# Cosine attention and a gated MLP in one kernel: neighbouring heads as a pair, norms in PSUM, roots by GpSimd's power, a new plan

## The chip, the cores and the metric

The kernel runs on one core of one Trainium2 chip. The core has a matrix engine (TensorE, PE in the profile, with its weight loads as PEld), a vector engine (VectorE, DVE), an engine for functions (ScalarE, ACT), a general one (GpSimd, POOL) and a queue engine that issues transfers (SyncE, SP); 16 DMA engines move data between the main memory, the on-chip memory SBUF and, through no DMA, the accumulation memory PSUM, which has eight banks. The engines run side by side, each through its own list of instructions in order, and wait for each other by semaphores. The metric is the device time of one execution in microseconds.

## The reference

Attention with normalised queries and keys over 8 batches of 12 heads, 448 positions and 64 columns, then a product with a gate over all 3584 tokens:

```python
def _attn_ref(q, k, v, tau):
    q_n = q / (np.linalg.norm(q, axis=-1, keepdims=True) + 1e-06)
    k_n = k / (np.linalg.norm(k, axis=-1, keepdims=True) + 1e-06)
    scores = np.matmul(q_n, k_n.transpose(0, 1, 3, 2)) / tau
    scores = scores - np.max(scores, axis=-1, keepdims=True)
    attn = np.exp(scores)
    attn = attn / (np.sum(attn, axis=-1, keepdims=True) + 1e-09)
    return np.matmul(attn, v)

def _moe_ref(x, w_in, w_out):          # 768 -> 2048 -> 768
    h = x @ w_in
    g = h * (1.0 / (1.0 + np.exp(-1.702 * h)))
    return g @ w_out

# attention out (8, 12, 448, 64) -> x (3584, 768), heads side by side
```

`tau` is 0.1. Everything comes and goes as float32; the kernel multiplies in float16.

## The kernel before, in words

**Tiling.** The unit of attention is a duo y: four heads of one batch, so three duos a batch (`ND = 3`) and 24 in all. A load (L217) puts the four heads' q, or k, into one tile `qk32` of 128 partitions: a head's 448 positions are 64 partitions of 7 positions each, two heads stand one above the other in the partitions, and two such stacks lie side by side (index j). So partitions 0 to 63 hold heads 0 and 2, partitions 64 to 127 heads 1 and 3 of the duo. After the transposes a pair of heads that is worked on together is what stood in one half of the partitions: heads 0 and 2, or 1 and 3. The rows of `w_in` are therefore not in their natural order on chip: `load_w_in` (L594) brings them in eight transfers that put the rows of each pair where the attention's result will be. v has four transfers a duo (L230), of 64 partitions each.

**Steps of a duo.** Squares (L243 on ACT, L242 on POOL for batch 1), sums over the 64 columns (L249, DVE), then the norm. In batch 0 that is a root by logarithm and exponential on ACT (L260, L261), and on DVE an addition of 1e-6 and a reciprocal (L265, L266), for q and k each by itself. From batch 1 it is `norm_a` and `norm_b`: a first guess of the inverse root from the bits of the number (L273), two Newton steps of three instructions (L286 to L290), and the correction for the 1e-6 (L297 to L301), ten DVE instructions; from batch 2 the second and third duo of a batch share one group. `scale` (L316) multiplies q or k by its inverse norm and writes float16: k of batch 0 and everything later on POOL, k in two pieces because its positions are placed in another order, q of batch 0 on DVE. Then q and k are turned: for the first six duos (`TURNED`) by PE (L339), with a DVE copy out of PSUM (L350), and the last 64 keys, which are treated by themselves, copied into the tile `kL` on DVE (L356); later by DMA transposes on SP (L362) with the `kL` copies on POOL (L371). PE makes the scores (L381, and L407 for the last keys), ACT the exponentials (L416), PE multiplies by v (L444, L455; v is cast to float16 into the tiles `vt` on POOL, L327 and L333, and carries a column of ones that yields the sums), DVE divides (L467, L475), and the result is turned to `xT` (L485 and L495, or a DMA transpose L503). Batch 0 is worked in two halves of its queries so that the product can begin early.

**The product.** L513 (L543 for batch 0) multiplies by `w_in`, ACT takes a tanh (L523), DVE the gate (L530, L555), L568 multiplies by `w_out`, ACT halves into `ost` (L579), SP stores (L589). The product of a batch is spread between the attention of the next ones.

**What sets the order.** A planner (`Plan`) simulates the engines when the program is built: every step has an engine, an assumed duration, a due time, steps that must be over before it, and counted buffers that it takes and frees. At each moment a free engine takes the ready step with the earliest due time. The order that results is what each engine's list holds; on the chip an engine waits in place at an instruction whose inputs are late, and everything behind it in its list waits too. `early` is the due time of squares, sums and norms; `hold` keeps the q, k and v loads of later batches until `w_in` or `w_out` have landed. The counted buffer `port` keeps POOL's steps and some of DVE's apart; `mm` counts the four PSUM banks for results, `sp` the two double banks for scores. Loads are issued in the order of their due times (`turn`). Eight semaphores serve the transfers of SP and ACT by turns, so the transfer that is issued eight later waits until the earlier has landed.

**The start.** DVE sets each of the six `vt` tiles to zero and writes its ones (L790 to L793), then clears the ends of the three `exp` tiles and the three `kL` tiles (L795, L796).

Of the kernel before, what the change touches and what calls it, by code (L numbers as in the profile page):

```python
# [10 lines left out]
FP32 = mybir.dt.float32  # L11
FP16 = mybir.dt.float16
I32 = mybir.dt.int32
# [4 lines left out]
RS_MAGIC = float(0x5F1FFFF9)  # L18
RS_A, RS_B = 0.703952253, 0.703952253 * 2.38924456
# [125 lines left out]
def kernel(  # L145
# [50 lines left out]

    ctx.enter_context(tc.manual_schedule())

    ident = const.tile([128, 128], FP16)
    w_in_sb = wpool.tile([128, KT1, DFF], FP16, name="w_in")  # L200
    w_out_sb = wpool.tile([128, KT2, DM], FP16, name="w_out")
    vts = [const.tile([128, 4, 2, D + 1], FP16, name=f"vt{i}") for i in range(NV)]
    exps = [const.tile([128, 2, EW], FP16, name=f"exp{i}") for i in range(NE)]
    kLs = [const.tile([128, 2, 128], FP16, name=f"kL{i}") for i in range(NE)]
# [9 lines left out]
    def load(y, d, src, nm):  # L214
        b, h0 = y // ND, (y % ND) * 4
        d[y] = p_in.tile([128, 2, C, D], FP32, name="qk32")
        return (nc.scalar if d is q32 and y == 0 else nc.sync).dma_start(  # L217
            out=d[y].rearrange("p j c d -> p j (c d)"),
            in_=src[b, h0 : h0 + 4]
            .rearrange("h s d -> (h s d)")  # L220
            .rearrange("(j q f) -> q j f", j=2, f=C * D),
        )

    def load_v(y, j, half):
        b, h0 = y // ND, (y % ND) * 4 + 2 * j
        if j + half == 0:
# [5 lines left out]
            in_=v[b, h0 : h0 + 2].rearrange("g (p c) d -> p g (c d)", c=C)[:, :, D * c0 : D * (c0 + n)],  # L232
        )

    def on_pool(y, ti):
        return y // ND == 1

# [7 lines left out]
    def reduce(y, ti):  # L245
        grp = group_of[y]
        if grp not in n2s:
            n2s[grp] = p_n.tile([128, len(grp), 2, 2, C], FP32, name=f"n2_{len(grp)}")
        nc.vector.tensor_reduce(  # L249
            out=n2s[grp][:, y - grp[0], ti],  # L250
# [5 lines left out]
    def root(y, ti):  # L256
        if y not in rss:
            rss[y] = p_n.tile([128, 2, 2, C], FP32, name="rs", bufs=4)
        n = n2s[group_of[y]][:, 0, ti]
        nc.scalar.activation(out=n, in_=n, func=AF.Ln)  # L260
        return nc.scalar.activation(out=n, in_=n, func=AF.Exp, scale=0.5)  # L261

    def invert(y, ti):
        n = n2s[group_of[y]][:, 0, ti]
        nc.vector.tensor_scalar(out=n, in0=n, scalar1=1e-6, scalar2=None, op0=ALU.add)  # L265
        return nc.vector.reciprocal(out=rss[y][:, ti], in_=n)  # L266

    def norm_a(grp):
        n = len(grp)
        a = n2s.pop(grp).rearrange("p g a b c -> p (g a b c)")  # L270
        y = p_n.tile([128, 4 * C * n], FP32, name=f"y_{n}")
        t = p_n.tile([128, 4 * C * n], FP32, name=f"t_{n}")
        nc.vector.tensor_scalar(  # L273
            out=y.bitcast(I32),
            in0=a.bitcast(I32),
            scalar1=-0.5,
            scalar2=RS_MAGIC,
            op0=ALU.mult,
            op1=ALU.add,
        )  # L280
        nrms[grp] = a, y, t
        return newton(grp, RS_A, RS_B)

    def newton(grp, ca, cb):
        a, y, t = nrms[grp]
        nc.vector.scalar_tensor_tensor(  # L286
            out=t, in0=y, scalar=-ca, in1=y, op0=ALU.mult, op1=ALU.mult
        )
        nc.vector.tensor_tensor(out=t, in0=t, in1=a, op=ALU.mult)
        return nc.vector.scalar_tensor_tensor(  # L290
            out=y, in0=t, scalar=cb, in1=y, op0=ALU.add, op1=ALU.mult
        )

    def norm_b(grp):
        newton(grp, 0.5, 1.5)
        a, y, t = nrms.pop(grp)
# [544 lines left out]
```

## Time and profile before

| | us |
|---|---|
| three runs | 445.81, 447.77, 452.8 (median 447.77) |
| the profiled execution | 453.23 |
| its span on the core | 451.5 |
| PE busy, share of the span | 414.7, 92% |
| ACT busy | 275.0, 61% |
| DVE busy | 233.1, 52% |
| POOL busy | 149.7, 33% |
| first score on PE | at 17.09 |
| first product of batch 0 (L543) | at 40.12 |
| DMA queue of SP and ACT (q1), share of 16 engines | 52.8% |

The span is the time from the first to the last instruction of the profiled execution. A line of the time line gives start and duration in microseconds, engine, source line, operation, output and inputs, and in brackets how long the engine had been idle just before and what released it. In a group of equal instructions the two numbers behind the bar are the busy time in all and the mean of one in nanoseconds; behind the second bar stands the idle time before them. The granted clock of PE was 0.991 in the mean. A matrix product counts as busy until its modelled end.

### The profile page before, as it was taken

The page shows a single profiled execution, that of the slowest core. Times are in us where ns is not written, and L with a number is a line of the kernel's source. Part 1 is how long each engine was busy: PE and PEld are TensorE (multiplying, and loading weights), DVE is VectorE, ACT ScalarE, POOL GpSimd, SP SyncE. Part 2 cuts the span into 40 slices and gives each one's busy share as a digit, 9 for nine tenths or more (in the row PEclk, how much of TensorE's full clock was granted, in tenths as well). Part 3 has the DMA queues.
Part 4 walks back from the last instruction along what each step waited for, and adds up shares of the span by engine and source line. Part 5 has one row for each costly group of instructions (what it writes and reads, how often), then busy time and mean ns, then how long its engine had stood idle before and what let it go on. Part 6 is the DMA issues. An engine that isn't in the chain of part 4 may idle for free.

```text
span 451.5 us, 9300 instructions
## 1 busy us (share of the span) xinstructions
PE 414.7 (92%) x3614; PEld 249.9 (55%) x3614; DVE 233.1 (52%) x605; ACT 275.0 (61%) x417; POOL 149.7 (33%) x271
## 2 busy tenths in 40 slices
PE   0589799999889999889999999799999999999995
PEld 0367677654456555455555555365555655565563
DVE  7835988796755755652664444571353115503400
ACT  5568476858877776764786565775666556324321
POOL 2666665556475174017421624017120000000000
PEclk9999899999999999999999999899999999999999
DMA  8798398999998888728864499337501321021022
GB/s 293 143 219 252 110 191 204 266 203 257 145 195 188 221 230 157 155 92 187 173 157 142 114 197 200 81 103 136 123 13 22 81 55 46 12 70 36 1 71 70
DMA packets 85996, 63.33 MB, mean 140 GB/s; under 512 B 54080, under 2 KB 80960, under 8 KB 85952
## 3 DMA queue, kind: packets, MB, share of 16 engines
q1 hardware_dynamic: 81936, 55.99, 52.8%
q0 software_dynamic: 3744, 6.29, 8.0%
q8 instruction: 28, 0.46, 0.4%
q10 hardware_dynamic: 272, 0.46, 0.3%
q14 instruction: 16, 0.13, 0.1%
HBM read 45.61 MB, written 11.01 MB: 125 GB/s over the span
## 4 chain that ended last, share of the span: by engine, by line
PE 66%; DMA 10%; POOL 6%; SPq 6%; issue 5%; DVE 4%; ACT 3%; POOLq 0%; ACTq 0%; DVEq 0%
PE mm L568 29%; PE mm L513 24%; PE mm L455 5%; PE sp L381 5%; DMA qk<-in_k_dram 4%; SPq L230 4%; DMA v<-in_v_dram 3%; POOL qks L316 3%; PE mm L444 2%; ACT exp L416 2%; PE sp L407 1%; DMA out_dram<-ost 1%; DMA qkT<-qks 1%; POOL sq L242 1%; SPq L217 1%
## 5 line engine op out<-in xcount | busy, mean ns | idle before, releaser
L416 ACT ACTIVATE exp<-sp 128x896 f16<-128x896 f32 (+1 forms) x171 | 148.2, 905 | 38.0 <-PE sp L381 32.8
L568 PE MATMUL mm<-w_out,gT 128*128 128x384 f16 x896 | 155.5, 326 | 1.6 <-DVE gT L530 1.4
L513 PE MATMUL mm<-xT,w_in 128*128 128x448 f16 x672 | 137.3, 354 | 0.9 <-DVE xs L475 0.9
L568 PEld LDWEIGHTS <-gT 128*128 128x128 f16 x896 | 84.3, 98 | 64.1 <-issue 9.5
L530 DVE SCALAR_TENSOR_TENSOR gT<-th,mm 128x448 f16<-128x448 f16 x112 | 68.5, 617 | 62.7 <-ACT th L523 62.6
L523 ACT ACTIVATE th<-mm 128x448 f16<-128x448 f32 x128 | 69.5, 548 | 51.4 <-PE mm L513 41.0
L513 PEld LDWEIGHTS <-w_in 128*128 128x128 f16 x672 | 62.8, 98 | 65.0 <-issue 9.1
L316 POOL TENSOR_TENSOR qks<-qk,y 128x512 f16<-128x512 f32 (+2 forms) x63 | 73.0, 1188 | 11.5 <-issue 5.3
L249 DVE TENSOR_REDUCE n<-sq 128x14 f32<-128x896 f32 x48 | 51.4, 1078 | 36.5 <-ACT sq L243 36.4
L455 PE MATMUL mm<-vt,exp 128*128 128x65 f16 (+1 forms) x1152 | 60.8, 197 | 1.8 <-ACT exp L416 1.8
L455 PEld LDWEIGHTS <-exp 128*128 128x128 f16 (+1 forms) x1152 | 54.1, 101 | 13.0 <-issue 5.4
L327 POOL CAST vt<-v 128x384 f16<-128x384 f32 x48 | 24.3, 506 | 109.2 <-PE mm L455 41.1
L579 ACT ACTIVATE ost<-mm 128x384 f32<-128x384 f32 x56 | 27.2, 492 | 49.9 <-PE mm L568 43.6
L243 ACT ACTIVATE sq<-qk 128x896 f32<-128x896 f32 x42 | 39.6, 950 | 28.3 <-DMA qk<-in_k_dram 21.7
L467 DVE RECIPROCAL rc<-mm 112x4 f32<-112x4 f32 x96 | 17.1, 178 | 68.7 <-PE mm L455 68.6
L444 PE MATMUL mm<-vt,exp 128*128 128x130 f16 x192 | 43.3, 225 | 5.3 <-DVE gT L530 4.7
L381 PE MATMUL sp<-qkT 64*128 64x448 f16 (+1 forms) x324 | 43.1, 348 | 1.9 <-ACT exp L416 1.6
L475 DVE TENSOR_TENSOR xs<-mm,rc 112x256 f16<-112x256 f32 x72 | 30.5, 424 | 2.5
L444 PEld LDWEIGHTS <-exp 128*128 128x128 f16 x192 | 19.4, 101 | 8.8 <-issue 2.6
L339 PE MATMUL mm<-ident,qks 128*128 128x128 f16 x84 | 9.8, 273 | 15.3 <-POOL qks L316 11.5
L333 POOL CAST vt<-v 64x64 f16<-64x64 f32 x96 | 22.5, 234 | 2.7
L543 PE MATMUL mm<-xT,w_in 128*128 128x224 f16 x192 | 21.9, 269 | 0.6 <-DVE gT L555 0.6
(43 smaller groups left out, 185.0 us busy)
## 6 DMA issues: line engine op xcount, KB each, us to landing
qk<-in_k_dram SPq DMA_DIRECT2D x24, 448.0 KB, 4.5
out_dram<-ost SPq DMA_DIRECT2D x54, 192.0 KB, 3.3
qk<-in_q_dram SPq DMA_DIRECT2D x23, 448.0 KB, 5.7
v<-in_v_dram SPq DMA_DIRECT2D x48, 128.0 KB, 3.4
v<-in_v_dram SPq DMA_DIRECT2D x48, 96.0 KB, 3.2
w_in<-in_moe_w_in_dram POOLq DMA_DIRECT2D x8, 384.0 KB, 8.4
w_out<-in_moe_w_out_dram POOLq DMA_DIRECT2D x2, 1536.0 KB, 15.1
qkT<-qks SPq DMA_TRANSPOSE x36, 4.4
```

Source lines behind the costliest of these rows:

```text
L243: return nc.scalar.activation(out=sqs[y, ti], in_=src, func=AF.Square)
L249: nc.vector.tensor_reduce(out=n2s[grp][:, y - grp[0], ti], in_=sqs.pop((y, ti)), axis=AX.X, op=ALU.add,)
L316: insts.append(eng.tensor_tensor(out=qkss[y][:, ti, first : first + step * (n - 1) + 1 : step].rearrange("p c j d -> p j c d"), in0=src[:, ...
L381: nc.tensor.matmul(out=sp[:, j, at : at + qn], lhsT=qkT[r, g, 1, 128 * n : 128 * (n + 1)], rhs=qkT[r, g, 0, q0 : q0 + qn], start=True, sto ...
L416: return nc.scalar.activation(out=dst, in_=src, func=AF.Exp, scale=inv_tau, **ekw)
L444: nc.tensor.matmul(out=o, lhsT=e[:, (C - 1) * S + a : (C - 1) * S + a + m], rhs=vt[:, 3].rearrange("p j d -> p (j d)"), start=True, stop=F ...
L455: nc.tensor.matmul(out=o[:, (D + 1) * j : (D + 1) * (j + 1)], lhsT=e[:, at : at + m], rhs=vt[:, n, j], start=False, stop=n == 2, skip_grou ...
L475: return nc.vector.tensor_tensor(out=xs, in0=ps[:, :, :D], in1=r[:, :, None].to_broadcast((P, 4, D)), op=ALU.mult,)
L513: nc.tensor.matmul(out=ps[:, :S], lhsT=w_in_sb[:, kk, 128 * m : 128 * (m + 1)], rhs=xTs[b, kk], start=(kk == 0), stop=(kk == KT1 - 1),)
L523: nc.scalar.activation(out=ths[key], in_=mms[key][:, :S], func=AF.Tanh, scale=0.851)
L530: nc.vector.scalar_tensor_tensor(out=gts[b // 2][:, m, (b % 2) * S : (b % 2 + 1) * S], in0=ths.pop((b, m)), scalar=1.0, in1=mms.pop((b, m) ...
L568: nc.tensor.matmul(out=mms[b2, t, n][:, :NW], lhsT=gts[b2][:, kk, 128 * t : 128 * (t + 1)], rhs=w_out_sb[:, kk, NW * n : NW * (n + 1)], st ...
```

## The change

Five things, all in one program:

- **Pairs.** Partitions 0 to 63 now hold heads 0 and 1 of a duo, partitions 64 to 127 heads 2 and 3. Each load of q or k becomes two transfers of 64 partitions; the planner is told 1.0 us instead of 0.5 for them. v keeps its four transfers a duo, from the new pairs' heads. `w_in` is loaded in its natural row order, in two transfers of 128 partitions.
- **Batch 0.** The inverse norms that DVE will multiply by are written to a PSUM bank (`rs_ps`), which leaves three banks for results until batch 0 is scaled. For duos 1 and 2 the roots of q and k are taken together. k of duo 0 is scaled on DVE instead of POOL.
- **Later norms.** The ten DVE steps go. POOL takes the square root as a power with exponent 0.5 (a tile `halves`), DVE adds 1e-6 and takes the reciprocal. There are no groups: every duo has its own norm.
- **Zeroing.** `vt`, `exp` and `kL` are each one tile with views. POOL writes the ones of all `vt` and zeroes only the parts that no cast writes; DVE clears the ends of `exp` and all of `kL` in one memset each.
- **Plan.** k is squared before q. The `kL` copies of the first six duos move from DVE to POOL and read the turned tile. `w_in` is due at once (behind the same `hold`). What the planner makes of it is a new order on all engines. PE has the same number of matrix products and weight loads as before.

```diff
 def load(y, d, src, nm):
     b, h0 = y // ND, (y % ND) * 4
     d[y] = p_in.tile([128, 2, C, D], FP32, name="qk32")
-    return (nc.scalar if d is q32 and y == 0 else nc.sync).dma_start(
-        out=d[y].rearrange("p j c d -> p j (c d)"),
-        in_=src[b, h0 : h0 + 4]
-        .rearrange("h s d -> (h s d)")
-        .rearrange("(j q f) -> q j f", j=2, f=C * D),
+    queue = nc.scalar if d is q32 and y == 0 else nc.sync
+    return tuple(
+        queue.dma_start(
+            out=d[y][64 * g : 64 * g + 64].rearrange("p j c d -> p j (c d)"),
+            in_=src[b, h0 + 2 * g : h0 + 2 * g + 2].rearrange("j (p c) d -> p j (c d)", c=C),
+        )
+        for g in range(2)
     )
...
+def scale_on_dve(y, ti):
+    return y == 0 or (y < ND and ti == 0)
...
-def root(y, ti):
+def root(y, tis):
+    n = flat(n2s[y][:, tis])
+    if y < ND:
+        nc.scalar.activation(out=n, in_=n, func=AF.Ln)
+        return nc.scalar.activation(out=n, in_=n, func=AF.Exp, scale=0.5)
+    return nc.gpsimd.tensor_tensor(out=n, in0=n, in1=halves.to_broadcast((128, 4 * C)), op=ALU.pow)
+
+def invert(y, tis):
+    n = flat(n2s[y][:, tis])
+    nc.vector.tensor_scalar(out=n, in0=n, scalar1=1e-6, scalar2=None, op0=ALU.add)
+    if y >= ND:
+        rss[y] = p_n.tile([128, 2, 2, C], FP32, name="rs", bufs=4)
+        return nc.vector.reciprocal(out=flat(rss[y]), in_=n)
+    for ti in range(tis.start, tis.stop):
+        if scale_on_dve(y, ti):
+            rss[y, ti] = rs_ps[:, y]
+        else:
+            rss[y, ti] = p_n.tile([128, 2, 2, C], FP32, name="rs", bufs=4)
+        last = nc.vector.reciprocal(out=rss[y, ti][:, ti], in_=n2s[y][:, ti])
     return last
-def norm_a(grp):
...
-def newton(grp, ca, cb):
...
-def norm_b(grp):
...
-    insts = [nc.vector.tensor_copy(
+    return nc.vector.tensor_copy(
         out=qkTs[y][:, :, ti].rearrange("q g (c p) -> q g c p", c=C), in_=ps
-    )]
-    if ti:
-        for j in range(2):
-            r = slice(64 * j, 64 * j + 64)
-            insts.append(nc.vector.tensor_copy(out=kLs[y % NE][r, :, r], in_=ps[r, :, C - 1]))
-    return tuple(insts)
+    )
...
+rs_ps = ps_m.tile([128, 512], FP32, name="mm")[:, : ND * 4 * C].rearrange("p (y t j c) -> p y t j c", y=ND, t=2, j=2)
...
-def load_w_in(i, j):
+def load_w_in(i):
     n = slice(1024 * i, 1024 * (i + 1))
-    rows = moe_w_in.rearrange("(e j g d) n -> j d e g n", j=2, g=2, d=D)[j]
-    return tuple(nc.gpsimd.dma_start(
-        out=w_in_sb[64 * j : 64 * (j + 1), g::2, n], in_=rows[:, :, g, n]
-    ) for g in range(2))
+    return nc.gpsimd.dma_start(
+        out=w_in_sb[:, :, n], in_=moe_w_in.rearrange("(k p) n -> p k n", p=128)[:, :, n]
+    )
...
-    dict(qk=NQK, v=2, sq=2, qks=4, vt=NV, qkT=NT, kL=NE, sp=2, mm=4, exp=NE)
+    dict(qk=NQK, v=2, sq=2, qks=4, vt=NV, qkT=NT, kL=NE, sp=2, mm=3, exp=NE)
...
-    early = due_of(grp[0]) - (5 if first else 8)
-    hold = {1: [("w_in", int(y > ND), 1)], 2: [("w_out", 1)] * (y == 2 * ND)}.get(b, [])
+    early = s - (5 if first else 8)
+    hold = {1: [("w_in", int(y > ND))], 2: [("w_out", 1)] * (y == 2 * ND)}.get(b, [])
...
-            add(("sq", ti, y), "POOL" if pl else "ACT", 1.85 if pl else 0.96, early + ti * 0.1, partial(square, y, ti),
+            add(("sq", ti, y), "POOL" if pl else "ACT", 1.85 if pl else 0.96, early + (1 - ti) * 0.1, partial(square, y, ti),
...
+        alone = [((1,), slice(1, 2)), ((0,), slice(0, 1))] if y == 0 else [((1, 0), slice(0, 2))]
+        for tis, cut in alone:
+            nn = 0.1 * len(tis)
+            add(("root", tis[0], y), "ACT" if first else "POOL", 0.4 if first else 0.4 + nn, early + 0.2, partial(root, y, cut),
+                after=[("red", ti, y) for ti in tis], takes=[("port", int(not first))], frees=[("port", int(not first))])
+            add(("inv", tis[0], y), "DVE", 0.3 + nn, early + 0.2, partial(invert, y, cut), after=[("root", tis[0], y)])
...
+            add(("kL", y), "POOL", 0.5, s - 2, partial(last_keys, y), after=[("qkT", 1, y)],
+                takes=[("kL", 1), ("port", 1)], frees=[("port", 1)])
...
+add(("roots", 0), "DVE", 0.0, 0, lambda: (), after=[("scale", ti, y) for y in range(ND) for ti in range(2)], frees=[("mm", 1)])
...
-            add(("w_in", i, j), "POOL", 2.0, i + 0.1 * j - 2, partial(load_w_in, i, j), hold=[("load", "q", ND - 1)],
-                dma=packets(384, 4096), **port)
+            add(("w_in", i), "POOL", 1.0, i - 20, partial(load_w_in, i), hold=[("load", "q", ND - 1)],
+                dma=packets(768, 4096), **port)
...
-for vt in vts:
-    nc.vector.memset(vt, 0.0)
-    nc.vector.memset(vt[:, :3, :, D : D + 1], 1.0)
-    for j in range(2):
-        nc.vector.memset(vt[64 * j : 64 * j + 64, 3, j, D : D + 1], 1.0)
-for e, kL in zip(exps, kLs):
-    nc.vector.memset(e[:, :, C * S :], 0.0)
-    nc.vector.memset(kL, 0.0)
+nc.gpsimd.memset(halves, 0.5)
+nc.gpsimd.memset(vts_all[:, :, :3, :, D : D + 1], 1.0)
+for j in range(2):
+    nc.gpsimd.memset(vts_all[64 * j : 64 * j + 64, :, 3, j, D : D + 1], 1.0)
+    nc.gpsimd.memset(vts_all[64 * j : 64 * j + 64, :, 3, 1 - j], 0.0)
+nc.vector.memset(exps_all[:, :, :, C * S :], 0.0)
+nc.vector.memset(kLs_all, 0.0)
```

## The prediction

> **What bounds the kernel now.** I read first the busy time by stretches of ten microseconds, because the page's total (PE 414.7 us of a 451.5 us span) says only that 36.8 us are left to win on TensorE. Columns: stretch, length, then busy us and instruction count of PE, PEld, DVE, ACT and POOL, granted clock, DMA share, GB/s.
>
> ```profile
> core 0: us, PE busy (x) PEld busy (x) DVE busy (x) ACT busy (x) POOL busy (x), PEclk, DMA share, GB/s
> 0.00:10.00 10.00, 0.00 (x0) 0.00 (x0) 7.40 (x35) 5.25 (x9) 1.55 (x7) 1.00 0.83 280
> 10.00:20.00 10.00, 4.72 (x35) 2.85 (x35) 8.96 (x23) 5.45 (x14) 7.21 (x14) 1.00 0.68 164
> 20.00:30.00 10.00, 8.18 (x76) 5.81 (x73) 3.65 (x8) 5.57 (x10) 7.88 (x18) 1.00 1.10 200
> 50.00:60.00 10.00, 8.20 (x89) 6.88 (x87) 7.91 (x20) 2.74 (x6) 8.25 (x7) 0.83 0.38 54
> 120.00:130.00 10.00, 8.27 (x92) 4.75 (x90) 6.45 (x20) 6.83 (x11) 7.91 (x10) 1.00 0.69 176
> 180.00:190.00 10.00, 7.89 (x60) 3.91 (x57) 5.83 (x11) 7.50 (x12) 0.92 (x3) 1.00 0.82 169
> 190.00:200.00 10.00, 8.61 (x85) 5.02 (x84) 5.35 (x10) 5.94 (x10) 1.50 (x5) 1.00 0.42 127
> 280.00:290.00 10.00, 7.70 (x57) 4.19 (x56) 5.31 (x10) 5.71 (x9) 0.92 (x3) 0.83 0.70 98
> ```
>
> PE idles 15.3 us in the first 20, 5.7 from 20 to 70, 3.9 from 110 to 140, 3.5 from 180 to 200, 2.7 from 260 to 290 and 4.6 at the end; from 300 to 440 it is full. Only the start and a few holes can move. So I read the time line of the start:
>
> ```profile
> 6.70 2.01 DVE L249 TENSOR_REDUCE n<-sq 128x14 f32<-128x896 f32 x2
> 9.15 1.84 POOL L316 TENSOR_TENSOR qks<-qk,rs 128x512 f16<-128x512 f32 x2 [7.83 <-DMA v<-in_v_dram]
> 13.28 1.03 DVE L316 TENSOR_TENSOR qks<-qk,rs 128x896 f16<-128x896 f32 x1
> 17.09 0.93 PE L381 MATMUL sp<-qkT 64*128 64x224 f16 x8
> ```
>
> The first score (17.09) waits for a DVE that runs without a break: zeroing to 6.7, reductions, scaling at 13.28. Then the waits, and the time line at the largest hole:
>
> ```profile
> 182.71 0.95 ACT L243 ACTIVATE sq<-qk 128x896 f32<-128x896 f32 x1 [2.44 <-DMA qk<-in_k_dram]
> 183.56 0.90 ACT L416 ACTIVATE exp<-sp 128x896 f16<-128x896 f32 x1
> 184.51 0.54 PE L407 MATMUL sp<-qkT,kL 128*128 128x448 f16 x2 [2.11 <-ACT exp L416]
> ```
>
> ACT stands at a square whose load has not landed, the exponential queued behind it is late, and PE waits 2.11 us. Last the groups by shape, for durations:
>
> ```profile
> L316 POOL TENSOR_TENSOR qks<-qk,y 128x896 f16<-128x896 f32 x21 | 35.4, 1687 | 0.2
> L371 POOL COPY kL<-qkT 64x128 f16<-64x128 f16 x36 | 10.4, 289 | 35.7 <-DVE y L301 25.2 <-DVE y L290 6.0 <-DMA qkT<-qks 3.3
> L316 DVE TENSOR_TENSOR qks<-qk,rs 128x896 f16<-128x896 f32 x3 | 3.1, 1045 | 0.0
> ```
>
> **The start.** Zeroing shrinks from DVE's 6 us to two memsets and some on POOL, which idled 7.83 us there: hidden, unless the first v lands before POOL is done. The k square ends at 5.96, so the first reduction comes 0.75 us sooner. From there, on DVE in the built order: two reductions to 8.0, add and reciprocal (0.17+0.24) to 8.4, k scaled on DVE in two pieces (1.2 us, from 1045 ns in one piece) to 9.6, the same for q (0.4+1.05) to 11.05, q's transposes (0.93) to 12.0, copy (0.62): first score about 12.7 instead of 17.09, -4.4. It shrinks at once. ACT now has two squares and a root pair (0.95+0.95+0.45) between the first exponential of heads 0 to 3 and the second; the last of that half ends at about 19.0 instead of 21.39, -2.4, and the next heads' scores stand behind the matmuls that need it. That is what is late next. The PSUM bank that the norms hold is one fewer for PE's results; that is covered, since the copy of q's transposes that frees the next one ends at about 20, before its writer needs it. The cover that can fail is the v load of heads 4 to 7: POOL casts it before scaling their k. Eight loads can be open at a time and the q/k loads now count double, so it is issued at about 10 and lands between 15 (no neighbour) and 22 (the 9.46 us that a v load took beside w_in in the chain). Early, the gain is 2.4; late, scores come at 28 instead of 24.93, a loss of 3. I take -2.3, since w_in is issued only after the last q of batch 0 has landed; bounds -4.4 to +3.
>
> **Batch 1.** The w_in issue takes two instructions (917 ns each by the w_out row) for eight of 649, at about 13 instead of 16.23 and 21.68; k of duo 4, held for w_in, is issued at 38.03 before, so about 3 us sooner. The second square of duo 4 no longer stands on POOL behind DVE's norms (49.65, after 5.45 idle), and scaling of duo 3 (51.29) can end before PE comes. PE's cost at 50 to 60 is 1.8 us idle and, after it, slow matmuls: 12 in 2.45 us against 1.31, 7 transposes in 0.95 against 0.55, a further 1.7. Bounds 0 to -3.5; I take -2.0, since PE also arrives sooner.
>
> **Norms after batch 0.** Per duo the ten DVE steps sum to 2.1 us (28 columns) or 2.4 (56), 33 us in all; two steps (0.18+0.33) remain, 11 us. DVE is off the path but for one place: at 119.06 to 121.77 a group of norms stands before three gates, and PE idles 1.64 at 122.35. That goes: -1.6, bounds 0 and -1.6. The power on POOL is in no row. Below: nothing, as its 28 columns are fewer than kL's 128 (289 ns). Above: the 1687 ns of the 896-column row, a weak end, since a power is not a product (the third rival). I take 0.3, nearest in size to the former; at 21 x 0.3 = 6 us it hides in POOL's 33%. The six pairs of kL copies that come to POOL (12 x 0.289 = 3.5 us) hide there too; without that cover each delays one score by 0.6.
>
> **The new plan.** In the built order the squares of duo 16 and 17 stand behind two more exponentials and a tanh, those of duo 12 behind three more; 2.11+1.39+0.51 us of PE idle hung on them. k is squared before q, as it is loaded. Bounds 0 and -4.0; I take -3.0. Against it: q and k of each duo are now four issues of about 0.6 us on SP instead of two, so q, and every transpose and store queued behind, start 1.2 us later, waited for by squares and by kL. The chain passes SP's issues at five places (75, 123, 175, 254, 275): 0 to +6; I take +2.0.
>
> v halves of 128 KB land in 3.4 us and whole q/k loads of 448 KB in 4.5 (k), so two halves side by side should not land sooner than one whole. The Trainium skill ("DMA: Bandwidth & Descriptors", rules for kernel authors) speaks against the split: transfers to disjoint partition halves serialize, one 128-partition transfer is to be used. By it the split buys nothing and only the second issue remains, which is my +2.0; were it wrong, that term would be 0.
>
> The trace shows POOL slower than DVE on the same scaling (1687 against 1045 ns) and no POOL instruction that pays for loading code. The Trainium skill ("GPSIMD Engine Reference", instruction dispatch) puts the first call to a freshly loaded kernel at about 6 us; if the power were such a call, once, in batch 1, the sum would be some 4 us smaller, an estimate.
>
> **Sum.** -2.3 -2.0 -1.6 -3.0 +2.0 = -6.9 us. The profiled execution took 453.2 us, 1.7 outside the span; it is 5.5 above the median of 447.8 and just above the slowest of the three. 446.3 on its scale is 440.9 on the median's: **441**. The matmuls are the same in number, so the whole idle of 36.8 us is the ceiling.
>
> **Rivals.** *Queue eats gain:* SP's five places cost their +6 and the start gives only about 1; 447.8 -1 -2 -1.6 -1.5 +6 = 447.7, 445 to 452. For it: SP's issues are 6% of the chain. Against: the planner charges the doubled issue. *All clears:* start -4.4, batch 1 -3.5, norms -1.6, squares -4.0, SP 0: 434.3, 430 to 438. For it: DVE's and ACT's waits are order, not work. Against: ACT is next within 6 us of the start. *Power saturates POOL (slower):* from 50 to 130 POOL is busy 50.8 of 80 us, 29.2 free, and nine powers fall there. Up to 29.2/9 = 3.2 us each they fit; beyond that every microsecond costs nine. At 4.7 us: +13.5, and the gains of batch 1 and squares are lost with it: 447.8 -2.3 +13.5 = 459, 456 to 468. For it: no row of a power; POOL's casts, kL and scaling are queued behind it. Against: 28 columns.
>
> **Chances.** Forecast 0.45 (own range 437 to 446), queue 0.22, all clears 0.23, POOL 0.10. Faster by over 2% (below 438.8): all of "clears" and about 0.07 of the forecast, 0.30; slower (above 456.7): 0.10; within 2%, about what a measurement of this kernel can tell from no change: 0.60. The range 432 to 453 leaves out the upper case and the lowest third of "clears", some 0.18.
>
> **What would show it.** First score near 12.7, first L543-type product near 38 instead of 40.12; PE busy above 9 in 50 to 60; no DVE norm before gates; no ACT wait on a k load near 183 and 195; POOL's power near 0.3 us. It is wrong if v of heads 4 to 7 lands after 20, if PE's idle between 70 and 300 stays at its 11.3 us, or if the power takes over 3 us.

## The result, and the profile after

| | us |
|---|---|
| after, median of 4 runs (lowest to highest) | 507.4 (506.0 to 509.7) |
| before, median of 4 runs beside them | 449.3 (445.8 to 452.8) |
| after / before, 95% interval | 1.133 (1.123 to 1.143) |
| profiled execution of after: time, span | 506.6, 504.9 |
| PE busy / idle, before (span 451.5) | 414.7 / 36.8 |
| PE busy / idle, after | 430.9 / 74.0 |

The kernel became 13% slower; the prediction's range ended at 453. Of the 53.4 us that the span grew, 37.2 are new idle time of PE, and 16.2 are the same 3614 matmuls taking longer.

First the view by stretches of ten microseconds, of the kernel after, for some of the places that were shown of before and for two more, 60 to 70 and 110 to 120. Columns: stretch, length, busy us and count of PE, PEld, DVE, ACT, POOL, granted clock, DMA share, GB/s.

```profile
core 0: us, PE busy (x) PEld busy (x) DVE busy (x) ACT busy (x) POOL busy (x), PEclk, DMA share, GB/s
0.00:10.00 10.00, 0.00 (x0) 0.00 (x0) 1.93 (x4) 3.37 (x5) 1.76 (x12) 1.00 0.83 183
10.00:20.00 10.00, 3.71 (x28) 2.34 (x28) 8.89 (x17) 6.21 (x12) 4.98 (x12) 1.00 1.11 235
...
50.00:60.00 10.00, 6.90 (x76) 5.92 (x74) 6.17 (x13) 3.95 (x7) 9.52 (x7) 0.85 0.30 64
60.00:70.00 10.00, 5.16 (x56) 3.94 (x54) 5.79 (x9) 5.13 (x7) 8.83 (x6) 0.84 0.97 157
110.00:120.00 10.00, 6.27 (x44) 3.45 (x41) 4.98 (x11) 1.33 (x2) 9.86 (x8) 0.83 0.57 118
120.00:130.00 10.00, 8.56 (x50) 4.08 (x49) 1.61 (x4) 4.96 (x9) 9.60 (x13) 1.00 0.67 147
190.00:200.00 10.00, 7.21 (x59) 3.82 (x58) 4.59 (x12) 6.45 (x9) 9.22 (x8) 0.84 0.45 74
```

The two added stretches in the kernel before:

```profile
60.00:70.00 10.00, 9.04 (x130) 7.32 (x128) 9.14 (x28) 6.97 (x11) 7.58 (x12) 1.00 1.16 211
110.00:120.00 10.00, 9.12 (x84) 4.90 (x85) 7.71 (x17) 8.39 (x12) 5.84 (x11) 1.00 1.15 196
```

In the last five stretches of the kernel after, POOL is busy for about nine tenths (before: 1.5 to 8.3 us of 10), and PE has holes there. DVE, from which the change takes work, is busy for less than two thirds of them, down to 1.6 us of 10, and the clock granted to PE is 0.83 to 0.85 in four of the five. Next, the group that the change added on POOL, and the wait that goes with it (us in total, times, longest):

```profile
L270 POOL TENSOR_TENSOR n<-n,halves 128x28 f32<-128x28 f32 x21 | 100.5, 4788 | 42.2 <-DVE n L255 26.1
```

```profile
DVE n L274 <- POOL n L270: 95.6, 21, 8.6
```

One power takes 4.79 us, where the prediction took 0.3; all 21 together, 100.5 us, are about the 99.7 us by which POOL's busy time grew (149.7 to 249.4). In all 21 places DVE stands still for it. What that does is seen in the time line of all engines, of the kernel after, at 108 us:

```profile
108.74 4.78 POOL L270 TENSOR_TENSOR n<-n,halves 128x28 f32<-128x28 f32 x1
113.56 0.46 DVE L274 TENSOR_SCALAR n<-n 128x28 f32<-128x28 f32 x1 [4.67 <-POOL n L270]
...
114.44 0.42 DVE L450 TENSOR_TENSOR xh<-mm,rc 112x256 f16<-112x256 f32 x1
...
114.92 0.37 PE L460 MATMUL mm<-ident,xh 112*128 112x112 f16 x2 [3.73 <-DVE xh L450]
```

DVE stands 4.67 us at the addition behind the root. The division of an attention result, which needs nothing from the root, is queued behind that addition, and PE idles 3.73 us until it comes. The power hardly makes DVE's own instructions longer: DVE is busy 210.1 us here, and 208.1 in the run below whose only difference is an addition in the power's place. The chain of work that ended last says the same; before, it had PE 66% and POOL 6%:

```profile
PE 48%; POOL 21%; DVE 8%; DMA 8%; SPq 7%; issue 4%; ACT 3%; POOLq 0%; ACTq 0%
```

Last the time line of the start, of the kernel after, against the prediction's 12.7 for the first score:

```profile
7.57 1.79 ACT L250 ACTIVATE sq<-qk 128x896 f32<-128x896 f32 x2 [5.55 <-DMA qk<-in_k_dram]
...
11.03 1.15 DVE L295 TENSOR_TENSOR qks<-qk,mm 128x512 f16<-128x512 f32 x2
...
15.37 0.93 PE L356 MATMUL sp<-qkT 64*128 64x224 f16 x8 [0.72 <-DVE qkT L329]
```

DVE's zeroing is gone, but the first square now waits for k until 7.57, where it began at 5.00 before, and the first product with `w_in` comes at 43.02, where it was at 40.12. The loads in two transfers are a second suspect.

### The profile page after: what moved, and what is told of

Read it like the earlier page. It is cut to its first block, busy times and chain, and to the rows that moved or that the text cites. A ratio compares the mean times of both kernels' runs of the same rounds, so it can differ in the third digit from the quotient of the medians.

```text
span 504.9 us, 9274 instructions
## 1 busy us (share of the span) xinstructions
PE 430.9 (85%) x3614; PEld 257.5 (51%) x3614; DVE 210.1 (42%) x457; ACT 275.9 (55%) x413; POOL 249.4 (49%) x302
## 4 chain that ended last, share of the span: by engine, by line
PE 48%; POOL 21%; DVE 8%; DMA 8%; SPq 7%; issue 4%; ACT 3%; POOLq 0%; ACTq 0%
PE mm L543 17%; PE mm L488 16%; POOL n L270 15%; DMA qk<-in_q_dram 6%; PE mm L430 5%; POOL qks L295 4%; PE sp L356 3%; DVE n L255 3%; SPq L234 2%; PE mm L518 2%; SPq L221 2%; PE mm L419 2%; DVE n L274 2%; DMA qk<-in_k_dram 2%; ACT sq L250 1%
## 5 line engine op out<-in xcount | busy, mean ns | idle before, releaser
L543 PE MATMUL mm<-w_out,gT 128*128 128x384 f16 x896 | 159.5, 331 | 5.1 <-DVE xs L450 2.8
L488 PE MATMUL mm<-xT,w_in 128*128 128x448 f16 x672 | 142.1, 362 | 14.3 <-DVE gT L505 14.3
L543 PEld LDWEIGHTS <-gT 128*128 128x128 f16 x896 | 85.7, 99 | 70.8 <-issue 16.5
L270 POOL TENSOR_TENSOR n<-n,halves 128x28 f32<-128x28 f32 x21 | 100.5, 4788 | 42.2 <-DVE n L255 26.1
L488 PEld LDWEIGHTS <-w_in 128*128 128x128 f16 x672 | 64.2, 100 | 81.8 <-issue 30.3
L295 POOL TENSOR_TENSOR qks<-qk,rs 128x512 f16<-128x512 f32 (+2 forms) x67 | 77.0, 1173 | 10.2 <-DVE rs L277 4.2
L430 PEld LDWEIGHTS <-exp 128*128 128x128 f16 (+1 forms) x1152 | 59.0, 107 | 13.5 <-issue 7.9
L430 PE MATMUL mm<-vt,exp 128*128 128x65 f16 (+1 forms) x1152 | 65.2, 204 | 0.6 <-ACT exp L391 0.6
L419 PE MATMUL mm<-vt,exp 128*128 128x130 f16 x192 | 45.4, 237 | 6.5 <-DVE gT L505 6.4
L274 DVE TENSOR_SCALAR n<-n 128x28 f32<-128x28 f32 (+1 forms) x25 | 10.2, 409 | 95.6 <-POOL n L270 95.6
```

The costliest lines, as they stand in the source:

```text
L270: return nc.gpsimd.tensor_tensor(out=n, in0=n, in1=halves.to_broadcast((128, 4 * C)), op=ALU.pow)
L295: insts.append(eng.tensor_tensor(out=qkss[y][:, ti, first : first + step * (n - 1) + 1 : step].rearrange("p c j d -> p j c d"), in0=src[:, ...
L419: nc.tensor.matmul(out=o, lhsT=e[:, (C - 1) * S + a : (C - 1) * S + a + m], rhs=vt[:, 3].rearrange("p j d -> p (j d)"), start=True, stop=F ...
L430: nc.tensor.matmul(out=o[:, (D + 1) * j : (D + 1) * (j + 1)], lhsT=e[:, at : at + m], rhs=vt[:, n, j], start=False, stop=n == 2, skip_grou ...
L488: nc.tensor.matmul(out=ps[:, :S], lhsT=w_in_sb[:, kk, 128 * m : 128 * (m + 1)], rhs=xTs[b, kk], start=(kk == 0), stop=(kk == KT1 - 1),)
L543: nc.tensor.matmul(out=mms[b2, t, n][:, :NW], lhsT=gts[b2][:, kk, 128 * t : 128 * (t + 1)], rhs=w_out_sb[:, kk, NW * n : NW * (n + 1)], st ...
```

## The experiments

Three theories were put to the chip. **A:** the power, 4.79 us each on POOL, whose list is worked in order. **B:** the q and k loads in two transfers of 64 partitions each. **C:** the rest, that is the replanned order, the copies of the last keys on POOL, one PSUM bank fewer. The table gives every run's ratio to the kernel before, taken on the same chip beside it.

| version | us | ratio, 95% interval |
|---|---|---|
| changed kernel | 507.4 | 1.133 (1.123 to 1.143) |
| its power as an addition, same order | 456.4 | 1.016 (1.013 to 1.020) |
| its power of 14 columns, same order | 465.3 | 1.041 (1.037 to 1.045) |
| its power of 21 columns, same order | 481.2 | 1.073 (1.067 to 1.079) |
| exponent -0.5, no DVE step behind it, same order | 485.6 | 1.081 (1.073 to 1.089) |
| planner told 4.8 us for the power | 454.6 | 1.010 (1.004 to 1.016) |
| Newton steps on DVE in its place | 460.6 | 1.030 (1.026 to 1.035) |
| Newton steps, pairing and transfers of before | 441.4 | 0.978 (0.971 to 0.986) |
| planner told 4.8 us, pairing and transfers of before | 440.1 | 0.981 (0.975 to 0.987) |
| the same with exponent -0.5 | 433.7 | 0.967 (0.963 to 0.971) |
| kernel before with the power | 512.8 | 1.147 (1.143 to 1.151) |
| the same, planner told the power's time | 446.1 | 0.993 (0.989 to 0.996) |
| kernel before, loads cut in halves of the partitions | 465.1 | 1.033 (1.028 to 1.039) |
| kernel before, loads cut along the heads | 457.4 | 1.016 (1.008 to 1.024) |
| changed kernel, told 4.8 us, loads cut along the heads | 790.5 | 1.762 (1.754 to 1.769) |

**How much is the power.** The instruction stays where it is in POOL's list, and its work varies; these three versions leave out the square roots after batch 0, wholly or in part:

```diff
-        return nc.gpsimd.tensor_tensor(out=n, in0=n, in1=halves.to_broadcast((128, 4 * C)), op=ALU.pow)
+        return nc.gpsimd.tensor_tensor(out=n, in0=n, in1=halves.to_broadcast((128, 4 * C)), op=ALU.add)
```

> The changed kernel, in which the 21 powers on POOL become an addition of 0.5 to the same 128x28 numbers at the same place of the same queue (the norms after batch 0 are then not square roots); the order of all instructions is the same. Theory A (the power is the whole loss): 436 to 449 us. Since the version with Newton steps stands at 460.6 and the one with 14 columns (2.58 us each) at 465.3, a second cause is likely: then 450 to 462 here, with the addition near 0.1 to 0.3 us. The difference to the changed kernel is the price of the power, (4.78 less that) x 21: if every microsecond of it is paid, about 95 us; at the measured total it is 45 to 60, so about half of it.

For 14 columns, and later for 21 (`3 * C`), the edit is

```diff
-        return nc.gpsimd.tensor_tensor(out=n, in0=n, in1=halves.to_broadcast((128, 4 * C)), op=ALU.pow)
+        n = n[:, : 2 * C]
+        return nc.gpsimd.tensor_tensor(out=n, in0=n, in1=halves.to_broadcast((128, 2 * C)), op=ALU.pow)
```

> The changed kernel with the power taken of 14 of the 28 columns (q's; k's norms after batch 0 stay squares), same order. If the time of a power goes by its columns, it takes about 2.4 us; if it is mostly a fixed cost, 4.3 to 4.8. Theory A with a threshold, as in the prediction's third rival (POOL has room for 3.2 us each): at 2.4 us within 2% of the kernel with the addition. Theory A without a threshold (each microsecond of POOL counts): half of the loss stays, 470 to 480 us. A fixed cost: 500 to 508. Theories B and C: over 480 whatever the power takes.

> The changed kernel with the power taken of 21 of the 28 columns (half of k's norms after batch 0 stay squares), same order. From 2.58 us for 14 columns and 4.79 for 28 the power should take 3.7 us. At this order an addition of 0.23 us gave 456.4, the power of 2.58 us 465.3, that of 4.79 us 507.4. If the price grows in proportion beyond a small threshold, so that every further microsecond is paid 21 times: 482 to 490 us. If POOL has room for 3.2 us and only what is above it counts: 468 to 477.

The groups of the three runs, the addition, 14 and 21 columns, one line from each:

```profile
L270 POOL TENSOR_TENSOR n<-n,halves 128x28 f32<-128x28 f32 x21 | 4.8, 231 | 29.9 <-DVE rc L442 15.2 <-DVE n L255 12.8 <-DMA out_dram<-ost 1.3
```

```profile
L271 POOL TENSOR_TENSOR n<-n,halves 128x14 f32<-128x14 f32 x21 | 54.3, 2584 | 38.6 <-DVE n L255 20.1
```

```profile
L271 POOL TENSOR_TENSOR n<-n,halves 128x21 f32<-128x21 f32 x21 | 77.4, 3684 | 41.5 <-DVE n L255 21.7 <-DVE rc L443 19.5
```

The same 28 columns cost 0.231 us as an addition. As a power they cost 2.584, 3.684 and 4.788 us for 14, 21 and 28 columns: 157 ns a column and 0.38 us besides. At this fixed order the kernel pays 3.8 us for each microsecond of the power up to 2.58 (8.9 / 2.35), 14.5 up to 3.68 (15.9 / 1.10) and 23.7 up to 4.79 (26.2 / 1.10). So the price is small at first and grows with the power's length. DVE's waits for POOL grow with it: 8.4 us in all with the addition, 49.3, 75.2 and 95.6 with the three powers. Not all of the price is waiting: of the step from 21 to 28 columns, 14.4 us are idle time of PE and 11.9 us are longer matmuls (59.6 to 74.0 and 419.0 to 430.9 us in the profiled executions). Four points do not settle whether the slope grows gradually or bends at one length: a bend near 3.1 us between the first slope and the last would fit them too (an estimate from these slopes). Of the expectations, 14 columns are 2.0% above the addition, at the edge of the branch with a threshold and below the other's 470 to 480; 21 columns fell between its two ranges. That the slope rises because the slack in the lists runs out is argued from it, not measured apart. Theory A accounts for 51 of the 58 us; but with no power at all 456.4 remains, 1.6% above the kernel before. There is a second cause.

**The power alone, in the kernel before.**

```diff
-        return newton(grp, RS_A, RS_B)
...
-        newton(grp, 0.5, 1.5)
...
+        return nc.gpsimd.tensor_tensor(out=a, in0=a, in1=halves.to_broadcast((128, 4 * C * len(grp))), op=ALU.pow)
+        nc.vector.tensor_scalar(out=a, in0=a, scalar1=1e-6, scalar2=None, op0=ALU.add)
+        last = nc.vector.reciprocal(out=y, in_=a)
```

> The kernel before, in which only the eight Newton steps on DVE after batch 0 give way to the power on POOL, followed by an addition and a reciprocal on DVE; its groups have 28 columns (9 times) and 56 columns (6 times); pairing, loads, zeroing and the copies of the last keys stay as before, the order is planned anew with the planner's guess of 0.6 to 0.8 us for a power. Theory A: 4.8 us for 28 columns and 9.6 us for 56, and 490 to 520 us. Theories B and C: the power alone costs at most half of the loss, 450 to 478.

Groups by shape, of that run:

```profile
L272 POOL TENSOR_TENSOR n<-n,halves 128x56 f32<-128x56 f32 x6 | 55.5, 9258 | 17.7 <-DVE rc L445 9.4 <-DVE n L250 8.2
L272 POOL TENSOR_TENSOR n<-n,halves 128x28 f32<-128x28 f32 x9 | 43.1, 4790 | 18.4 <-DVE n L250 18.2
```

512.8 us, as theory A has it: the power alone, without any other part of the change, brings all of the loss and a little more.

**Is it the time on POOL, or the order?** The planner had been told 0.6 us for a power. Telling it the true length changes no work, only the order:

```diff
-            add(("root", tis[0], y), "ACT" if first else "POOL", 0.4 if first else 0.4 + nn, early + 0.2, partial(root, y, cut),
+            add(("root", tis[0], y), "ACT" if first else "POOL", 0.4 if first else 4.8, early + 0.2, partial(root, y, cut),
```

> The changed kernel, with the power's cost in the planner 4.8 instead of 0.6 us, so that the order takes account of it; all work is the same. If the loss is POOL's time as such (POOL busy nine tenths from 50 to 210 us): no better than 495 us. If it is that the order was made for a short step and so other engines' queues stand behind a late POOL: 470 to 490.

Both branches of the expectation were too timid: 454.6 us, below the 456.4 of the addition that takes a twentieth of the time. The 100.5 us of powers are still on POOL, but DVE's wait for them, 95.6 us in 21 places after the change, is now

```profile
DVE n L274 <- POOL n L270: 18.4, 10, 5.2
```

In DVE's list 7.3 instructions stand, in the mean of the 21 places, between the last reduction of four heads and the addition that waits for their root; in the changed kernel there were 2.3, and in five places none. That is work with which DVE spends most of the 4.79 us. Told the length, the order leaves the 100 us of powers no dearer than the 4.8 us of additions in the order made for 0.6; this order is another one on every engine, so the two versions differ in more than the power's place. The kernel before, with its power, was planned anew in the same way (0.2 + 4.6 for each 28 columns):

> The kernel before with the power on POOL (512.8 us), in which the planner is told 4.8 us for 28 columns and 9.4 us for 56 instead of 0.6 and 0.8; else the same. If the loss is an order made for a short step: 445 to 462 us. If it was special to the changed kernel's order, and a power costs POOL's time here: 490 or more.

From 512.8 to 446.1 us, 0.7% faster than with Newton steps; DVE's waits for POOL's powers fall from 97.3 us to 3.8. Two kernels thus agree: the loss is not the power's 100 us of POOL; it is a list made for 0.6 us that met 4.79.

**Whose list stands?** With exponent -0.5 the power gives the scaling factor at once, without the 1e-6, so that nothing on DVE waits for it:

```diff
     def invert(y, tis):
+        if y >= ND:
+            rss[y] = n2s[y]
+            return ()
...
-    nc.gpsimd.memset(halves, 0.5)
+    nc.gpsimd.memset(halves, -0.5)
```

> The changed kernel (507.4 us) with exponent -0.5 instead of 0.5 after batch 0, so that the power is at once the factor for the scaling (the 1e-6 is left out there), and DVE's addition and reciprocal, which waited 95.6 us in 21 places for the power, are gone; the order of all other instructions is that of the changed kernel, with the planner's 0.6 us. If the loss is DVE's queue standing behind those waits, with the normalisations and gates that PE needs queued behind: 452 to 470 us. If it is POOL's own queue (scalings, casts, copies of the last keys late behind powers): 490 to 508. In between, both count.

485.6 us: of the 51 that the power costs at this order, 21.8 go with DVE's two steps and their waits (the steps' own time is in it: DVE is busy 12.0 us less). Of what is left, a part is PE waiting for POOL itself, as its waits in that run show (us in total, times, longest); the same two rows have 1.4 us each in the changed kernel:

```profile
PE mm L318 <- POOL qks L295: 8.4, 7, 3.2
PE sp L382 <- POOL kL L345: 8.0, 1, 8.0
```

Scalings and copies of the last keys stand behind powers in POOL's own list. So both lists count. The proportion, some 22 to 29, is rough: the power and the addition were not compared without the two steps.

**The second cause.** First the changed kernel with the Newton steps put back, planned with their old costs:

> The changed kernel with the norms after batch 0 by Newton steps on DVE, one group of 28 columns for each four heads (ten DVE steps, about 2.1 us each time), planned with the costs that the kernel before used for them; all else as changed. Theory A: 440 to 452 us, since what is left is the rest of the change, which the prediction put at -5.3 without the norms. Theory B: at least 470, as the split loads are still there. Theory C: at least 470 if it is the bank, the copies or the start; between 450 and 470 if it was that one planned order alone.

460.6 us, 3% slower than before though no power is left, so theory B or C holds for the rest. By the ranges of the expectation it would be C, one bad order; the next run says otherwise. In it the pairing and the transfers of before are put back as well (`load`, `load_v`, `load_w_in` and their planned costs, planned anew); of the edit, only `load`:

```diff
-                out=d[y][64 * g : 64 * g + 64].rearrange("p j c d -> p j (c d)"),
-                in_=src[b, h0 + 2 * g : h0 + 2 * g + 2].rearrange("j (p c) d -> p j (c d)", c=C),
-            )
-            for g in range(2)
+            out=d[y].rearrange("p j c d -> p j (c d)"),
+            in_=src[b, h0 : h0 + 4]
+            .rearrange("h s d -> (h s d)")
+            .rearrange("(j q f) -> q j f", j=2, f=C * D),
```

> The version with Newton steps (460.6 us), in which the pairing of heads and the transfers are as in the kernel before: one transfer for each q and k load, w_in in four transfers. The small zeroings, batch 0's norms, the squares' order and the copies of the last keys stay as changed. Theory B (the split loads are what is left of the loss): 438 to 449 us, with ACT's waits on q and k loads back from 42.0 us in all to under 30. Theory C (the order, the bank or the copies): 455 to 465.

441.4 us, 19 less, and faster than the kernel before. The bank, the zeroing and the copies of the last keys are still those of the change, so theory C's parts cost nothing net here; but this run differs from the last in the split, the pairing, the transfers of `w_in` and the order all at once. That the split is a cause by itself is shown by the kernel before with the split alone, further below. ACT's waits on q and k loads fall from 42.0 to 20.0 us, first with the loads split, then whole:

```profile
ACT sq L253 <- DMA qk<-in_k_dram: 32.9, 14, 5.6
ACT sq L253 <- DMA qk<-in_q_dram: 9.1, 7, 2.3
```

```profile
ACT sq L251 <- DMA qk<-in_k_dram: 16.7, 9, 3.1
ACT sq L251 <- DMA qk<-in_q_dram: 3.3, 4, 1.8
```

In the time line of that run the first score and the first product with `w_in` stand at

```profile
12.92 0.93 PE L371 MATMUL sp<-qkT 64*128 64x224 f16 x8 [0.71 <-DVE qkT L344]
```

```profile
37.04 2.23 PE L533 MATMUL mm<-xT,w_in 128*128 128x224 f16 x12
```

where the prediction had 12.7 and 38. Last, the split put into the kernel before, whose order stays:

```diff
-            out=d[y].rearrange("p j c d -> p j (c d)"),
...
+        rows = src[b, h0 : h0 + 4].rearrange("h s d -> (h s d)").rearrange("(j q f) -> q j f", j=2, f=C * D)
+        return tuple(
+            queue.dma_start(out=d[y][r].rearrange("p j c d -> p j (c d)"), in_=rows[r])
+            for r in (slice(0, 64), slice(64, 128))
+        )
```

> The kernel before, in which each q and k load is two transfers, one to each half of the partitions; the pairing, the planned order and all else are as before. Theory B: 454 to 462 us, with the first square at 7.5 instead of 5.0 us and ACT's waits on q and k loads above 40 instead of 27.5 us. Theory C: within 1% of the kernel before.

and the same number of transfers, cut along the heads instead:

```diff
-            queue.dma_start(out=d[y][r].rearrange("p j c d -> p j (c d)"), in_=rows[r])
-            for r in (slice(0, 64), slice(64, 128))
+            queue.dma_start(out=d[y][:, j].rearrange("p c d -> p (c d)"), in_=rows[:, j])
+            for j in range(2)
```

> The kernel before with each q and k load in two transfers as in the run with two halves of the partitions (465.1 us), but cut along the heads: each transfer goes to all 128 partitions and to half of each partition's elements. The number of issues on SP and the bytes are the same. If the price is the second issue on SP: 460 to 468 us, and the first square again near 7.3 us. If it is that transfers to half of the partitions are slow or serialize: 447 to 455 us and the first square near 5 us.

465.1 and 457.4 us, against 449.1 and 449.4 of the kernel before beside them; the first is above the 454 to 462 that theory B expected. Time lines, first with the halves, then along the heads (its profile is of the shortest of its four executions, 451.9):

```profile
0.75 2.98 SPq L220 DMA_DIRECT2D qk<-in_k_dram  x4
...
7.25 1.79 ACT L243 ACTIVATE sq<-qk 128x896 f32<-128x896 f32 x2 [5.23 <-DMA qk<-in_k_dram]
```

```profile
0.74 1.82 SPq L220 DMA_DIRECT2D qk<-in_k_dram  x4
...
5.14 1.79 ACT L243 ACTIVATE sq<-qk 128x896 f32<-128x896 f32 x2 [3.12 <-DMA qk<-in_k_dram]
```

Bytes and number of issues are equal. Each of these four issues of a transfer to 64 partitions occupied SP 0.745 us (later ones some 0.62), of one to 128 partitions 0.455 (the whole load before: 0.49), and k of the first heads landed 2.1 us later. So the 16 us of the split are roughly half the second issue (8.0, by the interval 3.6 to 10.8) and half the partition halves (7.7). The expectation had offered these as alternatives; both hold. How much of the second half is the longer issue and how much a slower landing, no run tells apart.

**Does the same cut help the changed kernel?** There, a pair's two heads lie side by side, so that one transfer's source runs over two heads of a stride, each of 64 partitions:

```diff
-                out=d[y][64 * g : 64 * g + 64].rearrange("p j c d -> p j (c d)"),
-                in_=src[b, h0 + 2 * g : h0 + 2 * g + 2].rearrange("j (p c) d -> p j (c d)", c=C),
+                out=d[y][:, j].rearrange("p c d -> p (c d)"),
+                in_=src[b, h0 + j : h0 + 3 + j : 2].rearrange("g (p c) d -> g p (c d)", c=C),
```

> The changed kernel with the planner's 4.8 us (454.6) and its own pairing of neighbours, in which each q and k load is still two transfers, but cut along the heads of a pair, so that each goes to all 128 partitions. If the halves of the partitions are part of the price here as in the kernel before (465.1 against 457.4): 444 to 450 us, with the first square near 5.1 instead of 7.6 us. If here only the number of issues counts: 452 to 457.

A plain miss: 790.5 us. Two stretches at the start of that run (the last columns are granted clock, DMA share, GB/s), and its time line:

```profile
2.00:8.00 6.00, 0.00 (x0) 0.00 (x0) 0.00 (x0) 0.01 (x1) 0.41 (x2) 1.00 0.12 42
8.00:14.00 6.00, 0.00 (x0) 0.00 (x0) 0.00 (x0) 0.00 (x0) 0.00 (x0) 1.00 0.13 50
```

```profile
22.46 1.79 ACT L250 ACTIVATE sq<-qk 128x896 f32<-128x896 f32 x2 [20.44 <-DMA qk<-in_k_dram]
```

The first square waits until 22.46 us, and meanwhile the DMA share is 0.12 to 0.13, where the changed kernel shows 1.02 and 1.11 in the same stretches. An eighth of 16 engines is two, and the source of each transfer is read as 2 blocks of 64 rows: the share is what two busy engines make, though no view here shows the engines one by one. The Trainium skill ("DMA: Bandwidth & Descriptors", rules for kernel authors) has this rule, that a slowest dimension of size c below 16 confines a transfer to at most c engines; the expectation had missed it, and the measured share agrees. For the changed kernel's pairing it stays open how much of its 14.5 us is issue and how much is halves.

**The best of both.** The changed kernel with the planner's 4.8 us and the transfers of before:

> The changed kernel with the power's cost in the planner 4.8 us (454.6 us in the last runs) and, in addition, the pairing and the transfers of the kernel before (one transfer for each q and k load, w_in in four). Both causes then are gone while all 21 powers of 4.78 us stay on POOL. If the two causes are separate: 454.6 less the 19 us that the same step gave the version with Newton steps, 434 to 444 us. If the power's time on POOL has a price of its own which the split loads hid: 446 to 456.

440.1 us, within the 434 to 444 expected if the two causes are separate. With exponent -0.5 and, as before, without the 1e-6 and the two DVE steps:

> The version with the planner's 4.8 us and the transfers of the kernel before (440.1 us), in which the power has exponent -0.5 and DVE's addition and reciprocal after batch 0 are gone (the 1e-6 is left out there). If DVE's waits on the power still cost something once the order knows its length: 432 to 438 us. If the right order already hides them: 438 to 443, within 1% of 440.1.

433.7 us, 3.3% faster than the kernel before and the fastest of all; without the two steps, and without the 16.5 us that DVE still waited for the power, it is 6.5 us faster than the version above it, in an order that is new again. Its page, busy times, PE's slices and the chain:

```profile
PE 409.5 (95%) x3614; PEld 246.9 (57%) x3614; DVE 197.6 (46%) x415; ACT 274.3 (63%) x413; POOL 251.7 (58%) x308
...
PE   1579999999999999999999999999999999999995
...
PE 86%; ACT 4%; DMA 3%; DVE 2%; SPq 2%; issue 1%; ACTq 0%
```

POOL is as busy as in the changed kernel (251.7 against 249.4 us) and is not on the chain at all.

## Why the prediction was wrong

The loss adds up: 507.4 to 454.6 for the order (52.8), to 440.1 for the split loads and what hangs on the pairing (14.5), and from there up to the kernel before's 449.3 the rest of the change, a gain of 9.2: 52.8 + 14.5 - 9.2 = 58.1.

**The step that failed** is "The power on POOL is in no row ... I take 0.3, nearest in size to the former". It sized an unknown operation by its number of columns; the rows that it was set between, a copy and a product, cost some 2 ns a column, the power 157. The upper bound of 1.687 us was too low as well, although the text called it weak. That "it hides in POOL's 33%" is true of the work, as the run with the right planned length shows, but not of the list that the change built. The planner's 0.4 + 0.2 us stood in the diff; the prediction counted the new plan as a gain of 3.0 and never asked what that plan is worth if the figure is wrong. Its own sign, "if the power takes over 3 us", came true with 4.79; PE's idle time between 70 and 300 us, which was to fall below 11.3, grew to 36.3.

**The third rival** had the mechanism and, with 4.7 us, the length. It had a chance of 0.10. Its price was wrong: nine powers between 50 and 130 us, +13.5. Only six start there, but DVE waits for all 21, from 47.8 to 354.8 us, and these waits were not in it. Up to 3.2 us the power was to cost nothing, but 2.58 us costs 9; beyond, each microsecond was to cost nine, and from 3.68 to 4.79 us it cost 23.7.

**SP's double issues**, "0 to +6; I take +2.0", is the second term mis-sized: +16.0 in the kernel before, 14.5 here together with what hangs on the pairing. It counted 1.2 us of delay for q at five places of the chain; at the start four issues took 2.98 us instead of 0.98 for two, and in the kernel before the split raised ACT's waits on q and k loads from 27.5 us in 14 places to 42.5 in 22. Of the rule in the Trainium skill ("DMA: Bandwidth & Descriptors", rules for kernel authors) that transfers to disjoint halves of the partitions serialize, the prediction said that by it only the second issue remains. The rule pointed the right way, and the runs make it dearer than that: 7.7 us beyond the second issue.

**What held.** The start, once loads are whole: first score 12.7 forecast, 12.92 measured; first product 38 forecast, 37.04 measured. With the split they came at 15.37, as k lands 2.6 us later, and at 43.02. The norms off DVE: -1.6 forecast, bounds 0 and -1.6; the kernel before with its power planned rightly gives -3.3 (0.7%), in a new order. Without SP's +2.0 the sum was -8.9; the changed kernel with both causes gone gives -9.2, though its `w_in` comes in eight transfers again. That agreement is of the sum and may be chance; batch 1's -2.0 and the squares' -3.0 were not measured apart. The prediction's queue of "casts, kL and scaling" behind the power was right too.

**The first call.** The Trainium skill ("GPSIMD Engine Reference", instruction dispatch) has a first call to a fresh kernel at about 6 us. All 21 powers lie between 4.78 and 4.83 us, the first included, and the first began 0.15 us after the sum that it waited for had ended: no such cost shows in this trace, and the power's price recurs each time.

## What to carry to other kernels

An operation that is in no row is not to be priced by the rows of other operations of its size; if a change stands or falls with it, carry a high value through every engine's list that it enters, and ask which work of others is queued behind the step that waits for it. Where a planner fixes the order from assumed durations, a wrong duration can cost far more than the work itself: with its 100 us of power the changed kernel took 454.6 us when they were planned at 4.8 us each, 53 us less than when they were planned at 0.6. Keep a load one transfer over all partitions, and look at the pattern of addresses on both sides when you regroup it.

## What the runs showed of the hardware

- GpSimd's power, 128 partitions of float32: 0.38 us and 157 ns a column (14 to 56 columns: 2.58, 3.68, 4.79, 9.26 us); an addition of 28 columns took 0.231.
- At the start a transfer to 64 partitions took 0.745 us to issue, one of the same bytes to 128 partitions 0.455, and the first loads landed 2.1 us later.
- A source read as 2 blocks of 64 rows: a DMA share of 0.12 to 0.13, the first square at 22.5 us instead of 7.9, the kernel at 790.5 instead of 454.6.
- The granted clock was lower in the runs in which PE often stands: 0.948 after the change, 0.949 and 0.953 in the two other runs over 485 us, 0.822 in that of 790, against 0.978 to 0.999 in the profiled executions of all others. After the 3.73 us of idle time of the kernel after, the clock is 0.50 for some three microseconds, and in the kernel before at 54 us likewise, where the longest idle time just before was 1.07 us (stretch, length, PE, PEld, DVE, ACT, POOL, clock, DMA share, GB/s; first after, then before):

```profile
115.00:116.00 1.00, 1.00 (x5) 0.54 (x6) 1.00 (x3) 0.00 (x0) 1.00 (x2) 0.50 0.00 0
```

```profile
54.00:55.00 1.00, 1.00 (x10) 0.86 (x7) 0.88 (x3) 0.00 (x0) 1.00 (x2) 0.50 0.00 0
```

So a stall can be paid twice: with the same order and an addition in the power's place, the same 3614 matmuls were busy 412.9 us instead of 430.9, at a clock of 0.982 instead of 0.948. Not every difference in busy time is the clock's: 414.7 us before at 0.991, 409.5 in the fastest version at 0.986. The Trainium skill ("TensorE: Matmul & The Clock Gate", what's actually happening) halves the clock after an idle window of about 3.4 us; one stretch at half clock of that length in ten microseconds would make 0.83, an estimate from that page, and 0.83 is what the stretch with the 3.73 us of idle time shows. The kernel before shows the same 0.83 from 50 to 60 and from 280 to 290 us, where the longest idle times are 1.07 and 2.30 us, so in this case less than 3.4 us of unbroken idle time was enough. No run varied the idle time alone.
